# Retention and top-1 experts in one kernel: where the first expert's weights stand among the loads of queries, keys and values

## The chip, the core and the metric

The kernel runs on one core of a Trainium2 chip. The metric is the time of one execution on the device in microseconds (us). A core has five engines, each with an instruction stream of its own that it follows in order: TensorE (PE, products), VectorE (DVE), ScalarE (ACT), GpSimd (POOL) and SyncE (SP, which here only issues DMAs). DMAs are issued from SyncE, ScalarE and GpSimd and are carried by 16 DMA engines. Engines wait for each other, and for the landing of DMAs, by semaphores.

## The reference

Two parts, in float32. First retention over 8 batches, 8 heads, 576 positions, head size 64:

```python
scores = scale * np.matmul(q, k.transpose(0, 1, 3, 2))
Dmat = np.where(rel >= 0, gamma[:, None, None] ** rel[None, :, :], 0.0)
attn_out = np.matmul(scores * Dmat[None], v)
x = attn_out.transpose(0, 2, 1, 3).reshape(4608, 512)
```

Then a mixture of 8 experts on these 4608 tokens of 512 numbers. A token is computed only where its skip score is positive; then it goes to the expert with the greatest logit:

```python
do_compute = x @ w_skip > 0
e_idx = argmax(xc @ w_gate)          # xc: the tokens that are computed
h = np.maximum(xc[mask] @ w1[e], 0)  # 512 -> 1024
y[mask] = gate_w[mask, None] * (h @ w2[e])   # 1024 -> 512
out[do_compute] = xc + y
```

## The kernel before

**Retention, in 36 tiles.** A tile g is 128 positions of one batch (or 64 of each of two batches), all heads. Its queries, keys and values lie in one SBUF tile `u_g`, which two loads fill from `qkv`, each of 128 x 1024 numbers, 512 KB: `load_half(g, 0)` and `load_half(g, 2)` (the second is half as large for every ninth tile, the last one among them). There are 5 buffers for u. In round g of the loop, TensorE makes the scores of tile g + 1 (`psc`, `psq`), the state (`ps_s`) and the values (`pxt`) of tiles g and g - 1, and transposes what is finished (`px`); VectorE and ScalarE multiply by the decay and copy; GpSimd scales the keys (`kn`) and the values (`vs`). Round g asks for the second half of tile g + 3 behind a block of products, and for the first half of tile g + 4 at its end. ScalarE copies finished tokens to `xn` and writes them to `out` in DRAM.

**Routing beside it.** Each four tiles, logits are made, and from them VectorE makes a rank for each token (`route_a`, `route_b`, `slots`). After 24 tiles the expert with most tokens so far is chosen to go first (`choose_first`); its number is `lead_id`, and SyncE reads it into a register (L370), since the address of the weights depends on it. After 28 tiles `close_first` makes the list `gi` of this expert's first 256 tokens, and GpSimd gathers them from `out` into `xg0` by two indirect DMAs (L352).

**The first expert's weights** come in 8 chunks of 512 KB (`w_0_f`, f = 0 to 7; `load_w`, L161), each a piece of `w1` and a piece of `w2`. There are 4 buffers for raw chunks. A product in float32 is made of three products of parts: each chunk is split in a high part `whi` (a cast on ScalarE, L776) and a low part `wlo` (raw less high: on GpSimd in four pieces, L781, or on VectorE, L171). A buffer comes free when the low part is made. The loads of the first five chunks, AHEAD = 5, and their splits are asked for by `weights()`, once in each round from the time at which the register has its number. In each call one load is asked for. The split of a chunk is asked for two calls later, but no sooner than the gathers (`"first" in marks`), except for the first KFRONT chunks.

**Behind the loop** the gathered tokens are transposed (`pt_early`), split on ScalarE (`x`, L175) and VectorE (L176), and `up_early` multiplies them by chunks 0 to 2 (`ph_early`); the rest of the routing goes on between these. Then the experts follow one after the other, TensorE busy nearly without a break.

The order on TensorE is the order in which the code is written. The other engines are ordered by a scheduler, which keeps to dependencies, to what `keep_in_program_order` and `issue_after` pin, and to the order of the code otherwise.

Of the kernel before, what the change touches and what calls it, by code (L numbers as in the profile page):

```python
# [24 lines left out]
NT = NTOK // P  # L25
# [23 lines left out]
UAHEAD = UBUFS - LAG  # L49
# [7 lines left out]
NQD = P // QD  # L57
KCUT = 3
KRANK = 4
KFRONT = 1  # L60
KCOUNT = 3
CUT = 2 * P
EARLY = ("sc0", "sc1", "xt")
# [25 lines left out]
def kernel(  # L89
# [9 lines left out]
    nc = tc.nc  # L99
# [58 lines left out]
    def load_w(e, f, regs):  # L158

        t = wpool.tile([P, 2, NCC, P], F32, tag="w", name=f"w_{e}_{f}", bufs=4)  # L160
        marks["load"] = nc.sync.dma_start(t.rearrange("p m c i -> p (m c i)"), w[bass.ds(regs[e], 1), f].rearrange("o p c -> (o p) c"))  # L161
        return t

    def parts(t):
        return [wpool.tile([P, 2, NCC, P], F32R, tag=n, name=f"{n}_{t.name}") for n in ("whi", "wlo")]
# [287 lines left out]
    wq, hs, marks = {}, {}, {}  # L453
    regs = []
# [38 lines left out]
    with ExitStack() as actx:  # L493
# [19 lines left out]
        def load_half(g, s, after=None):  # L513
            if s == 0:
                u_t[g] = ap.tile([P, 4, NPR, P], F32, tag="u", name=f"u_{g}", bufs=UBUFS)
            n = 1 if s and g % NQ == HALF else 2
            half = nc.sync.dma_start(
                u_t[g][:, s : s + n].rearrange("p s a i -> p (s a i)"),
                qkv[g, s // 2, :, : n * DM],
            )  # L520
            if after is not None:
                tc.add_manual_dep(
                    half.ins,
                    after.name,
                    mybir.DependencyInfo(mybir.DependencyClass.Sync, mybir.DependencyReason.DATA),
                    reason="the second half begins behind a block of products",
                )
# [5 lines left out]
        for g, s in ((0, 0), (1, 0), (0, 2), (2, 0), (1, 2), (3, 0), (2, 2), (3, 2)):  # L533
            load_half(g, s)
            if (g, s) == (1, 2):
                nc.sync.dma_start(gt_sb[:, 0], gtab.rearrange("p (a q) -> p a q", a=NPR))
# [215 lines left out]
        added = []  # L752
        chunks = []
        held = []

        def queue_behind(piece, other):
            tc.add_manual_dep(
                piece.ins,
                other.ins.name,
                mybir.DependencyInfo(mybir.DependencyClass.NoSync, mybir.DependencyReason.DATA),  # L760
                reason="the first gathers are asked for in front of these",
            )

        def weights():

            if not regs:
                return
            n = len(chunks)
            chunks.append(None)
            if 0 <= n - 2 < AHEAD:  # L770
                held.append(n - 2)
            while held and (held[0] < KFRONT or "first" in marks):
                f = held.pop(0)
                t = chunks[f]
                hi, lo = wq[0, f] = parts(t)
                tc.keep_in_program_order(nc.scalar.copy(hi, t))  # L776
                behind = ranked[-1] if len(ranked) == len(GROUPS) - 1 else None
                for m in range(2):
                    for c in range(0, NCC, NCC // 2):
                        some = lambda x: x[:, m, c : c + NCC // 2]  # L780
                        piece = nc.gpsimd.tensor_tensor(some(lo), some(t), some(hi).bitcast(F32), ALU.subtract)  # L781
                        if f < KFRONT:
                            tc.keep_in_program_order(piece)
                        else:
                            queue_behind(piece, marks["first"])
                        if behind is not None:
                            tc.add_manual_dep(
                                piece.ins,
                                behind.ins.name,
                                mybir.DependencyInfo(mybir.DependencyClass.Sync, mybir.DependencyReason.DATA),  # L790
                                reason="VectorE's operations on the gates go first",
                            )
                            behind = None
            if n < AHEAD:
                chunks[n] = load_w(0, n, regs)

        def slots(t):
            slot_match(t)
# [58 lines left out]
        for g in range(NT):  # L857
# [6 lines left out]
            if g == GLATE:  # L864
                load_half(g + UAHEAD - 1, 0, last_product())
            if g and g + UAHEAD - 1 < NT:
                load_half(g + UAHEAD - 1, 2, last_product())
# [20 lines left out]
            if last >= 1:  # L888
                stage_c(last - 1)
            routing(0 if g == NT - 1 else 3 if g < starts[KCUT + 1] else 8)  # L890
            weights()
        g = NT
        if LAG:
# [6 lines left out]
        while len(chunks) < AHEAD + 2:  # L900
            weights()
# [512 lines left out]
```

## Time and profile before

| | |
|---|---|
| three runs | 389.59, 392.66, 393.16 us; median 392.66 |
| profiled execution | 390.34 us, span 388.6 us |
| busy: TensorE, VectorE, ScalarE, GpSimd | 95%, 71%, 47%, 39% of the span |
| moved by DMA | 106.15 MB, 273 GB/s in the mean |
| the tiles' loop ends, first expert begins | at about 143 us, 153 us of the span |

The span goes from the first to the last instruction; the time of the execution has 1.7 us around it. All times of day below are microseconds from the span's start. An engine's idle time costs only where it lies on the way to the end; TensorE is the engine with the most work.

### The profile page before, as it was taken

Reading aid. Unit: us, or ns where it says so; the run is one execution under the profiler, and the core shown is the slowest. Engines: PE = TensorE matmul, PEld = TensorE weight load, DVE = VectorE, ACT = ScalarE, POOL = GpSimd, SP = SyncE. Lnnn points to the kernel's source line nnn. Section 1 sums busy time; section 2 is a strip of 40 time slices with the busy share of each in tenths; the row PEclk is TensorE's granted clock in tenths of the full one; section 3 lists DMA queues with packets and bytes.
Section 4 is the critical chain, followed back from the end, with each engine's and each line's share of the span. In section 5 each row is a group of like instructions: output and inputs, shape, how many; then the busy total and the mean of one; then the engine's idle time right before and its main releaser. Section 6 shows DMA issues by size and latency. Waiting matters only on the chain. (4 is left out here: it accounts for less than half of the span.)

```text
span 388.6 us, 12328 instructions
## 1 busy us (share of the span) xinstructions
PE 367.6 (95%) x4886; PEld 334.5 (86%) x4886; DVE 276.0 (71%) x615; ACT 181.7 (47%) x369; POOL 152.5 (39%) x211
## 2 busy tenths in 40 slices
PE   7899998989999898999999999999999999999991
PEld 3678877777887776888899999999999999999991
DVE  3576677578579794877856767867878768687762
ACT  2464555355544576117445455445545545555311
POOL 5885855555475389260136000420322322002032
PEclk9999999999999999999999999999999999999997
DMA  8989997989999988257899768978899898776511
GB/s 305 404 281 375 394 351 270 347 299 341 320 359 331 313 319 260 63 128 252 261 317 262 264 212 276 327 228 303 275 278 329 249 336 313 233 253 228 142 68 61
DMA packets 49573, 106.15 MB, mean 273 GB/s; under 512 B 6102, under 2 KB 21206, under 8 KB 49511
## 3 DMA queue, kind: packets, MB, share of 16 engines
q1 hardware_dynamic: 40951, 85.81, 65.2%
q0 software_dynamic: 3232, 9.99, 7.9%
q10 hardware_dynamic: 5328, 9.52, 6.5%
q8 instruction: 40, 0.66, 0.7%
q14 instruction: 22, 0.18, 0.1%
HBM read 83.51 MB, written 22.28 MB: 272 GB/s over the span
## 5 line engine op out<-in xcount | busy, mean ns | idle before, releaser
L171 DVE TENSOR_TENSOR wlo_w<-w,whi_w 128x1024 fp32r<-128x1024 f32 x59 | 72.0, 1223 | 37.8 <-ACT whi_w L170 35.4
L170 ACT CAST whi_w<-w 128x1024 fp32r<-128x1024 f32 x59 | 61.7, 1050 | 33.1 <-PE py L465 32.4
L465 PE MATMUL py<-hlo,whi_w 128*128 128x336 f32 (+6 forms) x224 | 67.8, 303 | 0.0
L465 PE MATMUL ph<-xhi,wlo_w 128*128 128x336 f32 (+6 forms) x224 | 67.6, 302 | 0.0
L465 PE MATMUL ph<-xlo,whi_w 128*128 128x336 f32 (+6 forms) x224 | 67.5, 302 | 0.0
L465 PE MATMUL ph<-xhi,whi_w 128*128 128x336 f32 (+6 forms) x224 | 67.5, 301 | 0.0
L465 PE MATMUL py<-hhi,wlo_w 128*128 128x336 f32 (+6 forms) x224 | 67.5, 301 | 0.0
L465 PE MATMUL py<-hhi,whi_w 128*128 128x336 f32 (+6 forms) x224 | 67.4, 301 | 0.0
L1035 POOL DMA_INDIRECT out<-rs,sidx x17 | 21.2, 1245 | 84.0 <-DVE rs L1034 82.8
L624 POOL TENSOR_TENSOR vs<-u,tab_sb 64x256 f32<-64x256 f32 x72 | 46.7, 649 | 9.9 <-DMA u<-qkv 2.7
L602 POOL TENSOR_TENSOR kn<-u,tab_sb 128x512 f32<-128x512 f32 x32 | 33.8, 1057 | 42.5 <-DMA u<-qkv 18.9
L687 PE MATMUL pxt<-u,vs 128*64 128x128 f32 (+1 forms) x576 | 47.8, 269 | 1.6 <-issue 1.6
L473 ACT ACTIVATE hhi<-ph 128x336 fp32r<-128x336 f32 (+8 forms) x61 | 25.8, 423 | 45.3 <-PE ph L465 45.0
L590 DVE TENSOR_TENSOR u<-psc,tab_sb 64x256 f32<-64x256 f32 x72 | 30.3, 420 | 23.4 <-PE pxt L663 7.7
L594 ACT COPY u<-psc 64x256 f32<-64x256 f32 x64 | 23.4, 366 | 48.7 <-DVE u L590 45.6
L465 PEld LDWEIGHTS ph<-xhi,whi_w 128*128 128x128 f32 x224 | 42.3, 189 | 0.1
L465 PEld LDWEIGHTS py<-hlo,whi_w 128*128 128x128 f32 x224 | 42.2, 188 | 0.2 <-DVE hlo L474 0.2
L465 PEld LDWEIGHTS ph<-xlo,whi_w 128*128 128x128 f32 x224 | 42.3, 189 | 0.1
L465 PEld LDWEIGHTS py<-hhi,whi_w 128*128 128x128 f32 x224 | 42.3, 189 | 0.0
L465 PEld LDWEIGHTS ph<-xhi,wlo_w 128*128 128x128 f32 x224 | 42.3, 189 | 0.0
L465 PEld LDWEIGHTS py<-hhi,wlo_w 128*128 128x128 f32 x224 | 42.3, 189 | 0.0
L572 PE MATMUL psc<-u 64*64 64x128 f32 (+1 forms) x576 | 39.1, 272 | 2.3 <-DMA u<-qkv 2.1
(213 smaller groups left out, 780.7 us busy)
## 6 DMA issues: line engine op xcount, KB each, us to landing
u<-qkv SPq DMA_DIRECT2D x68, 512.0 KB, 6.6
w<-w SPq DMA_DIRECT2D x64, 512.0 KB, 5.5
out<-xn ACTq DMA_DIRECT2D x36, 256.0 KB, 5.8
hop<-xg SPq DMA_DIRECT2D x12, 256.0 KB, 5.2
xh<-hop SPq DMA_DIRECT2D x48, 64.0 KB, 4.9
hopy<-yp SPq DMA_DIRECT2D x24, 128.0 KB, 3.4
yr<-hopy SPq DMA_DIRECT2D x6, 512.0 KB
u<-qkv SPq DMA_DIRECT2D x4, 256.0 KB
```

The lines of the kernel that those rows point to most:

```text
L170: nc.scalar.copy(hi, t)
L171: nc.vector.tensor_tensor(lo, t, hi.bitcast(F32), ALU.subtract)
L465: nc.tensor.matmul(ps, x, y, start=first and n == 0, stop=last and n == 3 * len(terms) - 1)
L473: nc.scalar.activation(hi, ph, AF.Relu)
L572: nc.tensor.matmul(psc_t[g][c][halves[1 - j ^ c], a, : q.stop - q.start], u[halves[j], 1 - j, a, c * D : (c + 1) * D], u[halves[j], j, a, ...
L590: nc.vector.tensor_tensor(u_t[g][h, j, :, :D], near[h, :, :D], mt_sb[h].unsqueeze(1).broadcast_to([D, NPR, D]), ALU.mult)
L594: nc.scalar.copy(u_t[g][h, j, :, D:], near[h, :, D:])
L602: nc.gpsimd.tensor_tensor(kn_t[g].rearrange("p a (j i) -> p a j i", j=2), u_t[g][:, 3].rearrange("p a (j i) -> p a j i", j=2), tt_sb[:, k ...
L624: nc.gpsimd.tensor_tensor(vs_t[g][h, j], u_t[g][h, 2, :, j * D : (j + 1) * D], tt_sb[h, TV + g % NQ // 2, :].unsqueeze(2).broadcast_to([D, ...
L687: nc.tensor.matmul(pxt[halves[j], a, q], vs_t[g][:, j, a, :], u_t[g][:, j, a, q], start=False, stop=a == NPR - 1, skip_group_check=True,)
L1035: done = nc.gpsimd.indirect_dma_start(out=out, out_offset=bass.IndirectOffsetOnAxis(ap=idx, axis=0), in_=rs[:n], in_offset=None, bounds_ch ...
```

## The change

Three things. Loads of chunks are no longer issued one by one between the loads of u: chunks that are asked for are put in a list, `due`, and issued only from the round on that asks for the last half of u, behind that half (`issue_after(marks["half"])`). And KFRONT is 0: the split of chunk 0 stands no longer in front of the gathers but behind them, as those of the other chunks do.

```diff
-KFRONT = 1
+KFRONT = 0
...
-            half = nc.sync.dma_start(
+            half = marks["half"] = nc.sync.dma_start(
                 u_t[g][:, s : s + n].rearrange("p s a i -> p (s a i)"),
                 qkv[g, s // 2, :, : n * DM],
             )
...
         held = []
+        due = []
...
             if n < AHEAD:
-                chunks[n] = load_w(0, n, regs)
+                due.append(n)
+            while due and g + UAHEAD >= NT:
+                f = due.pop(0)
+                with tc.issue_after(marks["half"].ins):
+                    chunks[f] = load_w(0, f, regs)
```

The first place is SyncE at the last loads of u. The names are the tile's or the chunk's number and the buffer's (`u_33_2489` is tile 33, `w_0_0_2522` chunk 0 of the first expert); ISA sets an address from a register. Before:

```order
L517 DMA u_33_2489<-qkv 128x1024
L370 TENSOR_LOAD lead_id_125
L161 ISA
L161 DMA w_0_0_2522<-w 128x1024
L517 DMA u_33_2489<-qkv 128x1024
L517 DMA u_34_2602<-qkv 128x1024
L161 ISA
L161 DMA w_0_1_2633<-w 128x1024
L517 DMA u_34_2602<-qkv 128x1024
L517 DMA u_35_2693<-qkv 128x1024
L161 ISA
L161 DMA w_0_2_2719<-w 128x1024
```

SyncE in the changed kernel, from the same load on:

```order
L517 DMA u_33_2489<-qkv 128x1024 x2
L517 DMA u_34_2600<-qkv 128x1024 x2
L517 DMA u_35_2689<-qkv 128x1024
L517 DMA u_35_2689<-qkv 128x512
L370 TENSOR_LOAD lead_id_125
L161 ISA
L161 DMA w_0_0_2801<-w 128x1024
L161 ISA
L161 DMA w_0_1_2803<-w 128x1024
L161 ISA
L161 DMA w_0_2_2805<-w 128x1024
```

The reading of `lead_id` and three loads of weights have moved behind the five loads of u that stood between them. The load of chunk 4 needs the buffer of chunk 0.

The second place is GpSimd from the keys of tile 33 to the split of chunk 1, with the two gathers (`xg0<-out,gi0`). Before:

```order
L602 TENSOR_TENSOR kn_33_2669<-u_33_2489,tab_sb_146 128x512
L624 TENSOR_TENSOR vs_33_2689<-u_33_2489,tab_sb_146 64x256 x2
L781 TENSOR_TENSOR wlo_w_0_0_2522_2713<-w_0_0_2522,whi_w_0_0_2522_2712 128x256 x4
L602 TENSOR_TENSOR kn_34_2755<-u_34_2602,tab_sb_146 128x512
L624 TENSOR_TENSOR vs_34_2775<-u_34_2602,tab_sb_146 64x256 x2
L624 TENSOR_TENSOR vs_35_2874<-u_35_2693,tab_sb_146 64x256 x2
L352 DMA xg0_126<-out,gi0_2907 128x512 x2
L781 TENSOR_TENSOR wlo_w_0_1_2633_2918<-w_0_1_2633,whi_w_0_1_2633_2917 128x256 x4
```

GpSimd in the changed kernel:

```order
L602 TENSOR_TENSOR kn_33_2665<-u_33_2489,tab_sb_146 128x512
L624 TENSOR_TENSOR vs_33_2685<-u_33_2489,tab_sb_146 64x256 x2
L602 TENSOR_TENSOR kn_34_2742<-u_34_2600,tab_sb_146 128x512
L624 TENSOR_TENSOR vs_34_2762<-u_34_2600,tab_sb_146 64x256 x2
L624 TENSOR_TENSOR vs_35_2867<-u_35_2689,tab_sb_146 64x256 x2
L352 DMA xg0_126<-out,gi0_2900 128x512 x2
L782 TENSOR_TENSOR wlo_w_0_0_2801_2911<-w_0_0_2801,whi_w_0_0_2801_2910 128x256 x4
L782 TENSOR_TENSOR wlo_w_0_1_2803_2918<-w_0_1_2803,whi_w_0_1_2803_2917 128x256 x4
```

The four pieces of chunk 0's low part have moved behind the gathers.

The third place is ScalarE from the write of tile 31 to the copies of the gathered tokens (`x0`), in the changed kernel:

```order
L708 DMA out<-xn_31_2877 128x512
L777 CAST whi_w_0_0_2801_2910<-w_0_0_2801 128x1024
L777 CAST whi_w_0_1_2803_2917<-w_0_1_2803 128x1024
L777 CAST whi_w_0_2_2805_2924<-w_0_2_2805 128x1024
L192 ACTIVATE ex0_86<-ls_28_2974 128x4x8
L649 COPY sv_34_3002<-ps_s_163 128x256
L707 COPY xn_32_3010<-px_32_3005 128x512
```

Three casts stand in a row here. ScalarE goes on two rows later with chunk 3:

```order
L777 CAST whi_w_0_3_2807_3013<-w_0_3_2807 128x1024
L707 COPY xn_33_3043<-px_33_3038 128x512
L708 DMA out<-xn_33_3043 128x512
L777 CAST whi_w_0_4_2931_3046<-w_0_4_2931 128x1024
L707 COPY xn_34_3084<-px_34_3079 128x512
L175 CAST x0_127<-pt_early_0_3087 128x2x256
L708 DMA out<-xn_34_3084 128x512
L175 CAST x0_127<-pt_early_2_3094 128x2x256
```

Chunk 4's cast stands ahead of the copies of the gathered tokens, as it did before. The cast of chunk 0 stood ten rows further ahead before, behind the write of tile 29; the rows from chunk 1's cast on stand as they stood.

## Rows read from the trace of the kernel before

**Rows 1.** The page, part 1: busy us (share of the span) and instructions.

```profile
PE 367.6 (95%) x4886; PEld 334.5 (86%) x4886; DVE 276.0 (71%) x615; ACT 181.7 (47%) x369; POOL 152.5 (39%) x211
```

**Rows 2.** Timeline of TensorE, 130 to 154: start, us, instruction [idle before <-releaser].

```profile
130.73 0.28 PE L663 MATMUL pxt<-sq,u 64*64 64x64 f32 x4
...
134.86 0.33 PE L572 MATMUL psc<-u 64*64 64x128 f32 x2 [1.21 <-DMA u<-qkv]
...
140.00 0.28 PE L572 MATMUL psc<-u 64*64 64x64 f32 x2 [0.60 <-DMA u<-qkv]
...
150.37 1.10 PE L741 MATMUL pt_early<-ident,xg 128*128 128x128 f32 x7 [1.80 <-DMA xg<-out,gi]
...
153.02 0.48 PE L465 MATMUL ph_early<-x,whi_w 128*128 128x256 f32 x2
```

**Rows 3.** Timeline of SyncE, 118 to 156: DMAs that it issues.

```profile
124.95 0.36 SPq L161 DMA_DIRECT2D w<-w  x1
125.41 1.79 SPq L517 DMA_DIRECT2D u<-qkv  x2
...
133.61 0.33 SPq L517 DMA_DIRECT2D u<-qkv  x1
```

**Rows 4.** Waits of SyncE, 118 to 140: us in total, times, longest.

```profile
SPq L517 <- DMA u<-qkv: 3.2, 1, 3.2
...
SPq L370 <- DVE u L590: 2.6, 1, 2.6
```

**Rows 5.** Tile u, 123 to 142: issue to landing.

```profile
DMA to landing us min/median/max: 7.9/7.9/7.9
```

**Rows 6.** Stretches: busy us of each engine, granted clock, DMA share, GB/s.

```profile
124.00:130.00 6.00, 6.00 (x152) 5.36 (x152) 5.74 (x21) 2.54 (x7) 2.50 (x4) 1.00 0.77 224
130.00:142.00 12.00, 9.81 (x252) 8.04 (x250) 9.50 (x32) 7.97 (x17) 7.28 (x10) 1.00 1.01 389
```

**Rows 7.** Timeline of VectorE, 138 to 155.

```profile
140.89 0.44 DVE L344 TENSOR_SCALAR gi<-ids 128x2 int32<-128x2 f32 x1
...
151.64 1.29 DVE L176 TENSOR_TENSOR x<-pt_early,x 128x512 fp32r<-128x512 f32 x2 [3.16 <-ACT x L175]
```

**Rows 8.** Timeline of GpSimd, 130 to 160.

```profile
136.10 2.79 POOL L781 TENSOR_TENSOR wlo_w<-w,whi_w 128x256 fp32r<-128x256 f32 x4
...
142.21 1.29 POOL L624 TENSOR_TENSOR vs<-u,tab_sb 64x256 f32<-64x256 f32 x2 [0.91 <-DMA u<-qkv]
143.68 1.22 POOL L352 DMA_INDIRECT xg<-out,gi  x1 [0.17 <-POOL vs L624]
145.21 1.01 POOL L352 DMA_INDIRECT xg<-out,gi  x1 [0.31 <-DVE cb L207]
146.24 11.06 POOL L781 TENSOR_TENSOR wlo_w<-w,whi_w 128x256 fp32r<-128x256 f32 x16
```

**Rows 9.** Timeline of ScalarE, 130 to 153.5.

```profile
147.08 1.04 ACT L776 CAST whi_w<-w 128x1024 fp32r<-128x1024 f32 x1 [0.41 <-ACT xn L707]
148.53 0.58 ACT L707 COPY xn<-px 128x512 f32<-128x512 f32 x1 [0.40 <-DMA out<-xn]
151.03 0.58 ACT L175 CAST x<-pt_early 128x512 fp32r<-128x512 f32 x1 [1.92 <-PE pt_early L741]
```

**Rows 10.** Tile w, 90 to 180: issue to landing.

```profile
DMA to landing us min/median/max: 4.3/6.2/8.8
```

**Rows 11.** Tile w, 148 to 160: issue to landing.

```profile
DMA to landing us min/median/max: 4.3/4.3/4.3
```

**Rows 12.** Tile xg, 140 to 152: issue to landing of the two gathers.

```profile
DMA to landing us min/median/max: 4.5/4.8/5.1
```

**Rows 13.** Stretches at the end of the trace, columns as in Rows 6.

```profile
380.00:381.00 1.00, 0.86 (x8) 0.51 (x6) 0.98 (x2) 0.00 (x0) 0.00 (x0) 1.00 0.00 0
384.00:385.00 1.00, 0.00 (x0) 0.00 (x0) 0.00 (x0) 0.00 (x0) 0.47 (x1) 0.69 0.57 217
```

**Rows 14.** Timeline of TensorE, 0 to 9.

```profile
1.28 4.02 PE L117 MATMUL ps_m<-mc 128*128 128x512 bf16 x9 [1.28 <-DVE mc L111]
```

## The prediction, made before the changed kernel ran

> **What bounds the kernel now.** I read the page first: TensorE is busy for 367.6 of 388.6 us [rows 1], so almost any idle time of it that goes comes off the end, and any that is added goes on. The change touches only the stretch in which the last tiles of queries, keys and values meet the first expert, so I then read TensorE's timeline there. It has three idle times with a releaser of interest [rows 2]: 1.21 us before the scores of tile 34 and 0.60 us before those of tile 35, both for a load of u, and 1.80 us before the transposes of the first gathered tokens, for the gather. Together 3.61 us; that is the most that the change can give: 392.66 - 3.6 = 389.1 us.
>
> Why those loads of u are late is seen on SyncE's timeline and in its waits. SyncE stood 2.6 us for the value of lead_id [rows 4] before it issued the first weights at 124.95, and only behind that the second half of tile 33 and the first of tile 34 (126.87, the second of the pair) [rows 3]. That load landed 7.9 us later [rows 5], at 134.8, which is where the scores of tile 34 start. The second half of tile 35 had another wait of 3.2 us for a load to land [rows 4] and left at 133.61, though the products that it stands behind were over at 131.0 [rows 2]. In the table by stretch the DMA engines were 77% busy from 124 to 130 and full (1.01, 389 GB/s) from 130 to 142 [rows 6]: time was left unused, then everything came at once.
>
> **What is removed.** SyncE's order now has all of u in front of lead_id and the weights. The load of tile 34 leaves up to 2.6 us sooner and has one chunk less before it, which at 389 GB/s is 1.3 us; it needs 1.2 to be there in time. So the 1.21 goes. Tile 35's first half has two chunks less before it, 2.7 us, and needs 0.6 more than the 1.2 by which its user moves up; so that goes too. TensorE comes to the end of the tiles some 1.8 us sooner.
>
> **The gather moves more than that.** In the trace GpSimd could not ask for the gather until it had scaled the values of tile 35, which began at 142.21 behind a load of u; the first gather began at 143.68 [rows 8]. The list of tokens had been ready since 140.89 + 0.44 = 141.33 on VectorE [rows 7]. With u early, the list is ready about 1.2 sooner, at 140.1. The values: load at 131.0, landed 7.9 later at 138.9, 1.29 of work and 0.17 of wait [rows 8], so 140.4; were the load to take 8.8 [rows 10], 141.3. I take 140.5 for the first gather, 3.2 us sooner than now, between bounds of 140.1 and 141.3, and 143.7 if nothing of this comes true.
>
> **What is added: a chain that was hidden.** There are four buffers for raw chunks, so the fifth load waits until the low part of chunk 0 is made. Before, that was done at 136.10 + 2.79 = 138.9, in the shade of the tiles [rows 8]. Now it stands behind both gathers. And on ScalarE the high part of chunk 4 stands, as before, ahead of the copy of tile 34 and of the two copies that take the gathered tokens out of PSUM. Before, chunk 4 was there when ScalarE came to it: it was cast at 147.08, four microseconds before the tokens' copies at 151.03 [rows 9]. Now those copies wait for it. Counted from the start of the first gather, g:
> both gathers issued, 146.24 - 143.68 = 2.56; four subtractions, 2.79 [rows 8]; the fifth load to landing, see below, 4.6; cast 1.04, copy of tile 34 0.58, two copies of tokens of 0.58 each [rows 9]; the last subtraction on VectorE, half of 1.29 [rows 7], 0.65; and 0.09 until TensorE starts (152.93 to 153.02) [rows 2, 7]. Sum 13.5 us.
> With g = 140.5 the first products of the expert begin at 154.0; in the trace they begin at 153.02. So **1.0 us is lost**, although 3.6 us of idle time were there to be won.
>
> The landing of that load is the unknown. In the stretch the loads of weights took 4.3, 6.2 in the middle, 8.8 at most [rows 10]; the one that can be timed from 148 on, when the rush is over, took 4.3 [rows 11], and the gathers of that time 4.5 to 5.1 [rows 12]. The fifth load leaves at 140.5 + 5.35 = 145.9, beside the second gather and two writes of out; I take 4.6. With 4.3 and the earliest g the loss is 0.3; with 6.2 and the latest g it is 3.4.
>
> **What costs nothing, and under which cover.** The three casts of chunks 0 to 2 now stand in one row on ScalarE ahead of the copies of tiles 32 and 33; four loads in a row must land for them. That is covered: TensorE has to wait for the gather and then for the fifth chunk anyway. TensorE is ready at 142.0 (second gather) + 5.1 + 2.65 of work (150.37 to 153.02) = 149.8, so casts may run 4 us late before they count, except chunk 0, which must be cast when GpSimd is free at 143.1; a load that leaves at 132 and takes 8.8 has landed at 140.8 and is cast by 141.9. GpSimd makes five low parts in a row instead of four, 2.8 us more, but begins 3.2 sooner: the loads of chunks 5 to 7, which wait for these, stay where they are. ScalarE's copy of u for tile 33 no longer stands behind a cast, which takes up to 1.05 off VectorE's way to the list; that is in the 1.2. Behind 154 every engine does what it did, and TensorE is the bound to the end, so 1.0 stays 1.0.
>
> **The sum.** The profiled execution took 390.34, its span 388.6. With +1.0 it becomes 391.3. The three runs have a median of 392.66 (389.59 to 393.16), 2.3 above it, so against the median I forecast 392.66 + 1.0 = **393.7 us**.
>
> **Rivals.**
> *The clock falls.* TensorE now stands idle from about 149.8 to 154.0, 4.2 us. At the end of the trace its last product is in 380 to 381, and in 384 to 385 the granted clock is 0.69 in the mean [rows 13], so it fell from 2.4 to 1.2 GHz within four microseconds of idleness; the idle time of 1.80 was followed by no fall. How dear: the first nine products of the kernel took 4.02 us, 447 ns for 512 columns, which is the lower level [rows 14]; so at most half of 4.02, 2.0 us, until it is up again. The time is then 392.66 + 3.0 = 395.7. One fall in a trace doesn't tell whether 4.2 us will always do. The Trainium skill (TensorE: Matmul & The Clock Gate, section "HAM oscillation — how this bites in real kernels") speaks here against the change: it says that a wait for DMA between two bursts of products sends the engine back to half its clock. By that rule the forecast would be 395.7, without it 393.7; the trace agrees that idleness ends in a fall, not that this wait is long enough.
>
> *The gather comes no sooner (slower).* If the DMA engines are the true limit and u lands as late as now, g stays at 143.7, and the chain of 13.5 ends at 157.2: +4.2, or 396.8. For it speaks the share of 1.01 from 130 on, against it the 77% before [rows 6]. It decides from g = 139.5 on: each microsecond of g later than that is one lost.
>
> *The fifth chunk isn't the last to come (faster).* If the load lands so fast that the tokens' copies wait for the gather alone, TensorE starts at 149.8 and the time is 392.66 - 3.2 = 389.5. For this the load would have to land within half a microsecond; the shortest seen is 4.3. Smaller gains, to about -1, need g near 139 together with a landing of 4.
>
> **How the numbers follow.** Chances: forecast 0.60, clock 0.20, gather no sooner 0.12, faster 0.08. The runs shown differ by 0.9%, so about 1%, 3.9 us, is what a measurement of this kernel can tell from no change. Beyond it on the slow side lie the second rival, and the clock's fall where the load also takes 5.5 (392.66 + 1.9 + 2.0 = 396.6): 0.16. On the fast side hardly anything lies, since all idle time together is 3.6: 0.04. Within: 0.80. The range goes from 390.0, a small gain with the runs at their lower values, to 397.2, the latest g or the fallen clock.
>
> **What would show it.** In the profile after: no idle time for u before the scores of tiles 34 and 35; the first gather near 140.5; the fifth load of weights issued near 146; on ScalarE an idle time before the cast of chunk 4 that ends with its load, and the tokens' copies right behind; TensorE idle for some 4 us before ph_early; the granted clock tells the first rival. I am wrong if TensorE's products on ph_early begin before 152.5 or after 156.5, or if idle time moves to a place behind them.

## The result and the profile after

The changed kernel takes 393.24 us (median of 21 runs, 389.19 to 397.96) beside 390.28 for the kernel before (21 runs); the ratio is 1.0085 with a 95% interval of 1.0057 to 1.0113. Measured twice more, it came to 1.0040 (1.0002 to 1.0079) and 1.0064 (1.0029 to 1.0099). The kernel before, measured against itself in the same series as the 1.0040, gave 1.0027 (0.9983 to 1.0071), so that series alone tells little. By the three together the change costs 0.4 to 0.9%, some 1.6 to 3.3 us: slower, and within the 1% that the prediction set as its bound. The profile of the second measurement fell in an execution of 399.9 us, 6 us above its median, and is not used; its times are.

The profiled execution took 393.43 us, its span 391.7. TensorE's timeline around the place, the answer to [rows 2]:

```profile
135.89 0.33 PE L572 MATMUL psc<-u 64*64 64x128 f32 x2
...
140.59 0.27 PE L572 MATMUL psc<-u 64*64 64x64 f32 x2
...
143.95 0.33 PE L687 MATMUL pxt<-u,vs 128*64 128x128 f32 x2 [0.50 <-issue]
...
149.49 0.66 PE L705 MATMUL px<-ident,xt 128*128 128x128 f32 x4
149.98 1.13 PE L741 MATMUL pt_early<-ident,xg 128*128 128x128 f32 x8
...
152.58 0.22 PE L232 MATMUL ps_m<-mks,ones 128*128 128x24 bf16 x3
155.50 0.54 PE L465 MATMUL ph_early<-x,whi_w 128*128 128x256 f32 x2 [2.70 <-DVE x L176]
155.84 0.41 PE L465 MATMUL ph_early<-x,wlo_w 128*128 128x256 f32 x1
156.05 0.63 PE L465 MATMUL ph_early<-x,whi_w 128*128 128x256 f32 x2
```

The three idle times of [rows 2], 1.21 and 0.60 for u and 1.80 for the gather, are gone. In their place stands one of 2.70, for the gathered tokens. The two products with whi that follow take 0.63 us together. Before, they took 0.41:

```profile
153.46 0.41 PE L465 MATMUL ph_early<-x,whi_w 128*128 128x256 f32 x2
```

The granted clock shows why. Stretches of after, columns as in [rows 6] (length, then busy time of TensorE's products and weight loads, VectorE, ScalarE, GpSimd, then the clock):

```profile
149.00:155.40 6.40, 3.80 (x45) 2.67 (x45) 1.93 (x4) 3.29 (x6) 6.40 (x10) 1.00 0.78 244
155.80:159.20 3.40, 3.40 (x18) 3.40 (x17) 1.54 (x9) 1.17 (x2) 3.40 (x6) 0.50 0.94 313
159.30:162.00 2.70, 2.70 (x28) 2.65 (x28) 2.63 (x13) 0.61 (x2) 0.28 (x3) 1.00 0.13 52
```

The clock is at 2.4 GHz during the idle time, falls to 1.2 GHz a third of a microsecond after the products have begun, and stays there for 3.4 us.

Who was late is read backwards. VectorE's timeline (its list `gi`, as in [rows 7], and the last subtraction), then ScalarE's, the answer to [rows 9]:

```profile
141.79 0.17 DVE L344 TENSOR_SCALAR gi<-ids 128x2 int32<-128x2 f32 x1
...
154.16 1.29 DVE L176 TENSOR_TENSOR x<-pt_early,x 128x512 fp32r<-128x512 f32 x2 [3.86 <-ACT x L175]
```

```profile
147.90 0.58 ACT L707 COPY xn<-px 128x512 f32<-128x512 f32 x1
...
152.11 1.05 ACT L777 CAST whi_w<-w 128x1024 fp32r<-128x1024 f32 x1 [3.62 <-DMA w<-w]
153.06 0.58 ACT L707 COPY xn<-px 128x512 f32<-128x512 f32 x1
153.54 0.59 ACT L175 CAST x<-pt_early 128x512 fp32r<-128x512 f32 x1
```

ScalarE stood 3.62 us at the cast of chunk 4, with the copy of the last tile and both copies of tokens behind it. The load that it waited for left SyncE at 148.3 and landed 3.8 us later; two rows of the tile's answer for 147 to 150, and what SyncE waited for (118 to 150, the answer to [rows 4]):

```profile
L161 SPq DMA_DIRECT2D w<-w x1: 333/333/333, 148.3 to 148.3; - x1
...
DMA to landing us min/median/max: 3.8/3.8/3.8
```

```profile
SPq L161 <- POOL wlo_w L782: 4.7, 1, 4.7
...
SPq L370 <- DVE u L590: 0.4, 1, 0.4
```

It left late because chunk 0's buffer came free late. SyncE no longer stands 2.6 us for lead_id, only 0.4, but stands 4.7 for a low part. GpSimd, the answer to [rows 8]:

```profile
139.91 1.29 POOL L624 TENSOR_TENSOR vs<-u,tab_sb 64x256 f32<-64x256 f32 x2 [2.08 <-PE pxt L687]
142.89 1.22 POOL L352 DMA_INDIRECT xg<-out,gi  x1 [1.69 <-issue]
144.42 1.01 POOL L352 DMA_INDIRECT xg<-out,gi  x1 [0.31 <-issue]
145.44 13.78 POOL L782 TENSOR_TENSOR wlo_w<-w,whi_w 128x256 fp32r<-128x256 f32 x20
```

### The profile page after: what moved, and what is told of

Its sections match the earlier page's. It is cut to its first block, busy times and chain, and to the rows that moved or that the text cites. A ratio compares the mean times of both kernels' runs of the same rounds, so it can differ in the third digit from the quotient of the medians.

```text
span 391.7 us, 12328 instructions
## 1 busy us (share of the span) xinstructions
PE 370.7 (95%) x4886; PEld 336.9 (86%) x4886; DVE 275.9 (70%) x615; ACT 181.4 (46%) x369; POOL 152.4 (39%) x211
## 4 chain that ended last, share of the span: by engine, by line
PE 67%; DMA 15%; issue 10%; DVE 3%; POOL 2%; ACT 1%; SPq 1%; POOLq 0%; ACTq 0%
PE py L465 17%; PE ph L465 16%; DMA out<-rs,sidx 8%; PE pxt L687 7%; PE ps_s L638 5%; PE px L705 5%; PE psc L572 5%; PE pxt L663 3%; DMA u<-qkv 2%; PE pl L713 2%; PE psq L572 2%; DMA xg<-out,gidx 2%; PE pn L728 1%; PE ph_early L465 1%; DMA tab_sb<-tab 1%
## 5 line engine op out<-in xcount | busy, mean ns | idle before, releaser
L624 POOL TENSOR_TENSOR vs<-u,tab_sb 64x256 f32<-64x256 f32 x72 | 45.6, 633 | 9.8 <-PE pxt L687 3.1
L572 PE MATMUL psc<-u 64*64 64x128 f32 (+1 forms) x576 | 40.1, 273 | 0.9 <-issue 0.9
```

The source lines that it names most:

```text
L572: nc.tensor.matmul(psc_t[g][c][halves[1 - j ^ c], a, : q.stop - q.start], u[halves[j], 1 - j, a, c * D : (c + 1) * D], u[halves[j], j, a, ...
L624: nc.gpsimd.tensor_tensor(vs_t[g][h, j], u_t[g][h, 2, :, j * D : (j + 1) * D], tt_sb[h, TV + g % NQ // 2, :].unsqueeze(2).broadcast_to([D, ...
```

## The experiments

One table serves them all. It has the starts of five of TensorE's instructions in each profile: the scores of tile 28 (up to there TensorE's instructions are the same in all kernels), those of tile 35, the transposes of tile 34 (the last ahead of the gathered tokens), the first product of `ph_early`, and the first product of the second expert; then the last less the first, and the ratio of the times with its interval.

| kernel | tile 28 | tile 35 | tile 34 turned | ph_early | second expert | 28 to second | ratio |
|---|---|---|---|---|---|---|---|
| before | 110.00 | 140.00 | 147.67 | 153.02 | 189.79 | 79.8 | |
| c0, before again | 111.74 | 141.24 | 149.62 | 154.51 | 191.40 | 79.7 | 1.0027 (0.9983 to 1.0071) |
| after | 111.33 | 140.59 | 149.49 | 155.50 | 193.83 | 82.5 | 1.0085 (1.0057 to 1.0113) |
| d4, after again | 110.29 | 140.12 | 148.48 | 154.79 | 193.30 | 83.0 | 1.0064 (1.0029 to 1.0099) |
| e1, filler | 110.50 | 139.50 | 147.84 | 155.14 | 192.03 | 81.5 | 1.0081 (1.0050 to 1.0112) |
| e2, cast behind | 112.03 | 141.25 | 150.85 | 154.02 | 191.44 | 79.4 | 1.0044 (1.0007 to 1.0080) |
| e3, own buffer | 113.55 | 141.96 | 152.13 | 155.30 | 192.15 | 78.6 | 1.0032 (0.9993 to 1.0070) |
| d1, e2 and e3 | 112.95 | 142.46 | 151.93 | 155.10 | 192.68 | 79.7 | 1.0026 (0.9985 to 1.0068) |
| e4, split only | 111.56 | 141.35 | 149.54 | 156.78 | 196.19 | 84.6 | 1.0173 (1.0123 to 1.0222) |
| d2, e4 and own buffer | 112.80 | 141.38 | 150.35 | 153.52 | 191.60 | 78.8 | 1.0047 (1.0017 to 1.0077) |
| d3, d2 and cast behind | 113.01 | 142.49 | 150.48 | 155.97 | 194.06 | 81.1 | 1.0060 (1.0023 to 1.0097) |
| c2, loads spread | 114.62 | 143.50 | 151.85 | 156.94 | 195.32 | 80.7 | 1.0065 (1.0028 to 1.0103) |
| c3, loads only | 109.99 | 140.95 | 149.51 | 153.00 | 189.92 | 79.9 | 1.0037 (1.0001 to 1.0073) |

From the second expert on all are alike (191.0 to 191.3 us to the last product, 192.5 in d1); behind the last product 6.4 to 8.3 us more follow (7.8 in before, 6.8 in c0, 6.9 in after). Tile 28 begins anywhere from 110.0 to 114.6, and at two different times in the two profiles of the kernel before, so a difference of total times of single profiles says little; the column "28 to second" says more. It has one profile for each experiment; the two of before are 0.1 us apart, those of after 0.5.

**Theory and rivals.** The theory is the prediction's: the split of chunk 0 behind the gathers makes chunk 4's load late, and ScalarE meets its cast ahead of the tokens. Rivals: the loss is the clock's fall alone; it is the four loads in a row; or it lies ahead of the place, where the profile of before was faster by 1.3 us.

**e1: is it the clock?** After, with eight filler products ahead of the first `up_early`. They add work and change no result.

```diff
+        fill = pp.tile([P, 512], F32, tag="sc1", name="fill")
+        for _ in range(8):
+            nc.tensor.matmul(fill, ones, ones.unsqueeze(1).broadcast_to([P, 4, P]), start=True, stop=True)
         up_early(0)
```

> The changed kernel with eight products of 128x512 (bf16, on a matrix of ones, result used by nobody) on TensorE ahead of the first ph_early, in the idle time of 2.70 us that its trace shows there. My theory: of the loss of 0.85% a part is the fallen clock (the trace of the changed kernel shows half clock for 3.4 us right behind that idle time). Then the granted clock stays at 1.00 from 150 to 165, the products of ph_early run at their full pace (0.36 us per group of three against 0.64), and the ratio to the kernel before is 1.0085 less 1.4 us of 390, about 1.005. Rival, the fall is a consequence of something else or costs nothing since VectorE sets the pace there: ratio stays at 1.008 to 1.009.

Timeline of e1, and the stretch in which the clock of after was down:

```profile
151.00 1.89 PE L912 MATMUL fill<-ones 128*128 128x512 bf16 x8
155.14 0.51 PE L465 MATMUL ph_early<-x,whi_w 128*128 128x256 f32 x2 [2.25 <-DVE x L176]
155.48 0.28 PE L465 MATMUL ph_early<-x,wlo_w 128*128 128x256 f32 x1
155.60 0.41 PE L465 MATMUL ph_early<-x,whi_w 128*128 128x256 f32 x2
```

```profile
155.80:159.20 3.40, 3.40 (x31) 3.40 (x30) 3.19 (x14) 1.16 (x3) 2.99 (x7) 1.00 0.85 336
```

The clock stays up (1.00 in place of 0.50), and from `ph_early` to the second expert it takes 36.9 us, in place of 38.3 in after and 38.5 in d4. So the fall costs 1.5 us; before has 36.8 and 36.9. The 28-to-second time is 1.0 and 1.5 shorter than in the profiles of after, and still 1.8 longer than before: the clock is about half of the loss. The time itself, 1.0081, is the rival's figure (1.008 to 1.009), not the theory's 1.005: it doesn't show the gain, 0.4%, which is less than the width of the interval.

**e2 and e3: is it the cast of chunk 4, and its buffer?** In e2 chunk 4's split is asked for behind the copies of the tokens; in e3 it has a raw buffer of its own, so that its load waits for no one (a small tile, `gtr`, gets one buffer in place of two, for room).

```diff
-            while held and (held[0] < KFRONT or "first" in marks):
+            while held and "first" in marks and (held[0] < AHEAD - 1 or "turned" in marks):
...
         up_early(0)
+        marks["turned"] = True
+        weights()
```

```diff
-                    chunks[f] = load_w(0, f, regs)
+                    own = ac.tile([P, 2, NCC, P], F32, tag="w4", name="w_own") if f == AHEAD - 1 else None
+                    chunks[f] = load_w(0, f, regs, own)
```

> The changed kernel, but the split of chunk 4 is asked for behind the copies of the gathered tokens and the first ph_early, so that on ScalarE the tokens' copies no longer stand behind the cast that waits for the fifth load. My theory, that this place makes the loss: TensorE begins ph_early 2.7 us sooner against the last tile than in the changed kernel, the clock doesn't fall, and 2.7 + 1.4 = 4.1 us come back: ratio to before 0.998 (0.995 to 1.001). Rival, the loss lies in the rush of four weight loads on the last tiles: the ratio stays at 1.008, and the idle time goes elsewhere.

> The changed kernel, but chunk 4 has a raw buffer of its own, so that its load doesn't wait for the low part of chunk 0; the order on ScalarE is that of the changed kernel. My theory (the fifth load is late only because it waits for that buffer): it is issued right behind the fourth, near 138, has landed by 147, the cast of chunk 4 doesn't wait, and TensorE begins ph_early when the gather allows: as in the run before, ratio 0.998. Rival 1, a fifth load in the rush delays the last tiles or the gather: TensorE's wait moves to the gather, ratio near 1.003. Rival 2, the place isn't it: 1.008.

ScalarE in e2, where the copies of tokens come right behind that of the tile, and in e3, where the cast is still ahead of them but waits for no load:

```profile
151.54 0.59 ACT L707 COPY xn<-px 128x512 f32<-128x512 f32 x1 [1.70 <-PE px L705]
152.02 0.59 ACT L175 CAST x<-pt_early 128x512 fp32r<-128x512 f32 x1
```

```profile
151.54 1.05 ACT L777 CAST whi_w_own<-w_own 128x1024 fp32r<-128x1024 f32 x1 [0.41 <-ACT xn L707]
152.82 0.58 ACT L707 COPY xn<-px 128x512 f32<-128x512 f32 x1 [0.24 <-PE px L705]
153.31 0.59 ACT L175 CAST x<-pt_early 128x512 fp32r<-128x512 f32 x1
```

In both, `ph_early` follows the turned tile 34 by 3.17 us (6.0 and 6.3 in after, 5.3 and 4.9 in before), TensorE does not wait, the clock stays up. The whole loss of the stretch is gone: 79.4 and 78.6. That shows the chain: buffer, load, cast, copies. The times came out worse than the theories, which had 0.998 for both: 1.0044, and 1.0032, the figure of e3's first rival. What e2 and e3 win at this point over before, some 2 us, they lose ahead of it: from the scores of tile 35 to the turned tile 34 they take 9.6 and 10.2 us, before and c0 7.7 and 8.4. TensorE stands in the middle of a block of products, in e2 for

```profile
145.31 0.33 PE L687 MATMUL pxt<-u,vs 128*64 128x128 f32 x2 [1.61 <-issue]
```

and in e3 for 1.52, waiting for nothing that the profile shows; this is taken up by c2. The rest of what their times are above before lies outside the stretch (see c0).

**e4: the split alone.** Before, with KFRONT at 0; the loads stay between those of u.

```diff
-KFRONT = 1
+KFRONT = 0
```

> The kernel before with one part of the change alone, the split of chunk 0 behind the gathers; the loads stand where they stood. My theory: the fifth load waits for chunk 0's low part here too, and now without the earlier gather: first gather near 143.7 minus the 1 us that ScalarE no longer spends on a cast in between at best, ph_early 13.5 later, that is 3 to 4 us later than before, and the clock falls as well: ratio 1.010 to 1.014, worse than the change as a whole. Rival, that the moved loads make the loss: ratio near 1.000.

ScalarE, and the stretch behind the first products:

```profile
153.38 1.04 ACT L776 CAST whi_w<-w 128x1024 fp32r<-128x1024 f32 x1 [4.84 <-DMA w<-w]
```

```profile
155.70:162.40 6.70, 5.62 (x26) 5.62 (x27) 4.48 (x19) 2.51 (x5) 5.54 (x11) 0.50 0.66 235
```

This half alone loses more than the whole: ScalarE waits 4.84 us, TensorE 3.67, the clock is down for 6.8 us, and the time is 1.7% longer, more than the 1.0 to 1.4% expected.

**c3: the loads alone.** After with KFRONT at 1 (and the loads asked for ahead of the splits within `weights()`, since the first split is asked for in the same call).

```diff
-KFRONT = 0
+KFRONT = 1
```

> The changed kernel with KFRONT at 1: the loads stand behind those of u, but the split of chunk 0 stays in front of the gathers (the other half of the change alone). Theory: ScalarE waits for chunk 0 (landing about 139.5) ahead of its copies for tile 35, some 2.3 us, and GpSimd makes 2.8 us of low part ahead of the last values and the gathers, so the gathers are asked for about 2 us later than in after; chunk 4's buffer comes free 5 us sooner and its cast waits no more. From tile 31 to the second expert 69 to 71 us, 392 to 394.5 us in all. Rival: chunk 4's load was all that made the change slower, the earlier wait costs nothing, and this gives 67 us and about 391.

The rival was right (67.2 us from tile 31 to the second expert, 391.53 in all). ScalarE and GpSimd do wait for chunk 0 ahead of tile 35 (the row below is TensorE, at the scores of tile 35), but there is no wait for chunk 4, `ph_early` follows tile 34 by 3.5 us, and the stretch is 79.9, that of before.

```profile
140.95 0.27 PE L572 MATMUL psc<-u 64*64 64x64 f32 x2 [1.43 <-ACT lt L722]
```

So by the stretch the loads behind u win nothing by themselves, and all of the loss comes with the split. The times alone do not show it: in this series c3 has 1.0037, after 1.0040, and the kernel before itself 1.0027.

**c0: is it chance that before was ahead at tile 28?** The same kernel once more.

> The kernel before, unchanged. In the profiles so far the scores of tile 28 begin at 110.0 us in before and at 110.5 to 113.6 in after and the four experiments, though TensorE's instructions are the same up to there; the idle of TensorE that no release explains ('issue') up to tile 31 is 3.3 us in before and 3.3 to 5.6 in the others. If that is chance, this second profile of before begins tile 28 anywhere between 110 and 113.5, and the ratio to before is 1.000 within its interval. If the changed programs are slower from the start, it begins tile 28 at 110.0 within 0.5.

Tile 28 begins at 111.74 this time, c3 and d4 begin it at 109.99 and 110.29: that before was ahead of after was chance. For the kernels with a remedy chance is not shown. All six profiles of them (e2, e3, and c2, d1, d2, d3 below) begin tile 28 at 112.0 or later, the seven others at 111.7 or sooner; two of the six, d1 and c2, have a fall of the clock on the way. Whether a remedy makes the kernel slower there, which would explain the ratios above 1 of e2, e3, d1 and d2 beside stretches no longer than before's, no run tells. The waits for u that the change is about are a matter of this chance too. TensorE in c0:

```profile
136.34 0.33 PE L572 MATMUL psc<-u 64*64 64x128 f32 x2 [0.45 <-DMA u<-qkv]
...
151.85 1.11 PE L741 MATMUL pt_early<-ident,xg 128*128 128x128 f32 x7 [1.46 <-DMA xg<-out,gi]
```

Where [rows 2] have 1.21 and 0.60, there are 0.45 and none. The three other kernels whose loads stand between those of u show the same spread: none in e4 and d2, 1.22 in d3. What could be won here was nothing to 1.8 us from one execution to the next.

**c1 and d4: after again.**

> The changed kernel, unchanged. Theory: from the scores of tile 31 to the first product of the second expert it takes 69.6 us again (before: 67.8), with 2.7 us of idle time in front of the first products of the gathered tokens and the clock fallen behind it; what lies ahead of tile 31 is chance and may come out 0 to 2 us shorter. Time 391.5 to 393.5, ratio 1.005 to 1.010. Rival: the fall of the clock was a matter of that one execution; then 68.2 us and 391 to 392.

> The changed kernel, unchanged, a third profile. 82.5 to 83.5 us from the scores of tile 28 to the second expert as in the first two, with 2.4 to 2.7 us of idle time ahead of the first products of the gathered tokens and the clock fallen for 3.41 us right behind it; ratio 1.003 to 1.010. Rival: without a fall of the clock it is 81 us and a ratio under 1.004.

c1 gave 393.57 us, the ratio 1.0040 as above, less than expected. The profile of d4 is that of after again, with 3.00 us of idle time, more than expected, and the clock down from 154.85 on for 3.41 us:

```profile
154.79 0.78 PE L465 MATMUL ph_early<-x,whi_w 128*128 128x256 f32 x2 [3.00 <-DVE x L176]
```

The mean granted clock of the timed runs fits a fall there in most executions, not in all: its median is 0.995 for before, 0.990, 0.991 and 0.990 for the three measurements of after, 0.9945 for e1, 0.994 to 0.995 for e2, e3, d1, d2 and c3, and 0.9875 for e4. A fall of 3.4 us is 0.5 x 3.4 / 391 = 0.004. The mean doesn't tell where the clock fell.

**c2: are the four loads in a row to blame for the 1.6 us?** e2, with each of the loads of chunks 1 to 3 held until another round's products are done, and chunks 2 and 3 split behind the tokens as well.

```diff
+                if f:
+                    tc.add_manual_dep(
+                        marks["load"].ins,
+                        last_product().name,
...
+                if n < AHEAD + 1:
+                    break
...
-            while held and "first" in marks and (held[0] < AHEAD - 1 or "turned" in marks):
+            while held and "first" in marks and (held[0] < 2 or "turned" in marks):
```

> The kernel of e2 (cast of chunk 4 behind the token copies), with the loads of chunks 1 to 3 each held until the products of another round are done, in place of four loads in a row, and the splits of chunks 2 and 3 behind the token copies too. Theory: with four loads of weights in a row, TensorE stood still for 1.61 us at 145.3 in e2 and 1.52 in e3 in the middle of a block of products that waited for no one, 1.4 us behind the landing of a 16 KB packet of its instructions; without the rush this stall is under 0.3 us, the stretch from tile 31 to the second expert falls from 67.2 to 65.6 us, and the time from 392.4 to about 390.9. Rival: the loads have nothing to do with that stall, it stays at 1 us or more, and the time stays at 392.4. Third: chunk 2's late split holds up its products, and the time goes up.

The stall at that place is gone, and the time is no shorter all the same (1.0065 beside 1.0044). None of the three outcomes came as put: the wait moved to ScalarE, whose copy needs a buffer that an earlier write to `out` still reads.

```profile
154.50 0.59 ACT L707 COPY xn<-px 128x512 f32<-128x512 f32 x1 [3.79 <-DMA out<-xn]
```

Whether the loads in a row cause the stall stays open. With four in a row it was 0.50 and 0.36 (after, d4), 1.61 (e2), 1.52 (e3), 1.48 (d1), but under 0.2 in e1 and c3; without, 0.84 in d2 and 0.2 or less in before, c0, e4, d3 and c2.

**d1, d2, d3: does a mended version beat before?** d1 has both remedies. d2 is e4 with the buffer of its own, d3 is d2 with the cast behind the tokens; their edits are those of e2 and e3.

> The changed kernel with both remedies: chunk 4 has a raw buffer of its own (e3), and its split is asked for behind the copies of the gathered tokens (e2). From the scores of tile 28 to the first product of the second expert it takes 79.4 us with e2, 78.6 with e3, 82.5 in after, 79.8 and 79.7 in the two profiles of before. Theory: either remedy alone already takes the whole wait away (3.17 us from the last transposes of the tiles to the first products of the gathered tokens in both), so both together give 78.5 to 79.5 us, no fallen clock, and a time within 1% of before (ratio 0.996 to 1.004). Rival: each leaves a part, and both give under 78 us and a ratio under 0.996.

> The kernel of e4 (before with the split of chunk 0 behind the gathers, the loads of weights still between those of queries, keys and values), with a raw buffer of its own for chunk 4. e4 takes 84.6 us from the scores of tile 28 to the second expert. Theory: all that e4 loses comes from chunk 4's load, which waits for the buffer of chunk 0; with a buffer of its own this is 78.5 to 80 us, the clock does not fall, and the time is within 1% of before. Rival: the late low part itself holds up the first products; then it stays over 82 us and over 1% slower.

> d2 with chunk 4's split behind the token copies as well. Theory: the same as d2 within 0.7 us (78.5 to 79.5 us in the stretch, ratio 0.996 to 1.004). Rival: without the four loads in a row, TensorE does not stand still behind tile 35's scores (1.5 to 1.6 us in e2 and e3), and this is the version that beats before: 77.5 us and a ratio under 0.996.

None is shown to. d1 is as e2 and e3, 79.7 and 1.0026. d2 shows once more that e4's loss was the buffer: 78.8 in place of 84.6, 3.17 us from tile 34 to `ph_early`; its ratio, 1.0047, is clear of 1. Neither d3's theory nor its rival came true: 81.1 us. In d3 waits as in before are back, 1.22 for u and

```profile
153.32 1.11 PE L741 MATMUL pt_early<-ident,xg 128*128 128x128 f32 x7 [2.06 <-DMA xg<-out,gi]
```

for the gather. d2, whose loads stand in the same places, has neither. In e2, d1, d2 and d3 the way from `ph_early` to the second expert is 0.6 to 1.3 us longer than in before, with no fall of the clock; TensorE waits 0.46 to 0.99 us there for the routing (`mks`, VectorE).

## Why the prediction was right, and where it was not

It said 393.7 us in a range of 390.0 to 397.2, no difference beyond 1%; measured were 393.24 and ratios of 1.004 to 1.0085. The chain is the one that it named; the fall of the clock on top of it was one of its rivals, not the forecast. The sizes are not as forecast: it expected 1.0 us of loss above a median of 392.66, and the loss is larger, 3.0 us in the stretch (82.5 and 83.0 against 79.8 and 79.7), while that median of three runs was high: 390.28 in 21 runs. The two errors nearly cancel in the time; that the forecast lies 0.5 us from the measured median is luck. By its steps:

- *The waits for u go.* No wait for u is left there in any profile with the loads behind u, and in after SyncE stands 0.4 in place of 2.6 for lead_id. But e4 and d2 have none either, with the loads where they stood, so the moved loads are not shown to be needed for it. *TensorE comes to the end of the tiles some 1.8 us sooner*: wrong. From tile 28 to the scores of tile 35 it takes 29.3 and 29.8 us in after and d4, 30.0 and 29.5 in before and c0: 0.2 in the mean. One reason is that the 1.8 was one execution's (0.45 in c0), the other that idle time which waits for nothing shown is larger: in that stretch 1.6 and 2.6 us in after and d4, 1.0 and 1.7 in before and c0. And behind it, up to the turned tile 34, 0.6 more is lost.
- *The first gather 3.2 us sooner, at 140.5.* Mis-sized: 142.89. Counted from tile 28 it is 31.6 and 32.0 in after and d4 against 33.7 and 33.5 in before and c0, 1.8 us sooner. The values were no hindrance (done at 141.20), the list was: 141.79 + 0.17 = 141.96, in place of the 140.1 that the prediction took. And the gather began only 0.93 us behind the list; in all seven profiles of the table in which the list comes last (after, d4, e1, e2, e3, d1, c2) it is 0.93 or 0.94. The prediction had no such term: it counted only the 0.17 from values to gather.
- *The fifth load waits for chunk 0's low part; ScalarE's cast of it holds up the tokens.* Right, shown by e2, e3 and d2, which each cut the chain at another link.
- *13.5 us from the gather to the first products.* 12.61 in after and 12.46 in d4. The load took 3.8 in place of 4.6; the rest is as summed.
- *Three casts in a row cost nothing.* Neither shown nor disproved: products of after wait 0.33 us behind ScalarE there, but those of c0, without the row, wait 0.64 at the same place.
- *TensorE is ready at 149.8 and stands for some 4 us.* It is ready at 152.8, since the tiles end later, and stands for 2.70. With g mis-sized by 2.4 and the chain by -0.9, `ph_early` begins at 155.5, not 154.0: within the bounds that the prediction set itself (152.5 to 156.5).
- *The clock falls*, a rival with a chance of 0.20 and a price of up to 2.0 us. It is what happened in both profiles, and the price is some 1.5. The prediction took its measure from the end of the trace and judged a fall unlikely, at 4.2 us of idle time; it came at 2.70. The Trainium skill's rule, which it cited (TensorE: Matmul & The Clock Gate, "HAM oscillation — how this bites in real kernels"), that a wait between two bursts of products sends the clock to half, came true here: 0.50 from 155.8 on. The waits of the page's example are longer than this one, and not every wait here was followed by a fall: 1.80 us in before and 2.06 in d3 were not. The forecast's 1.0 for the chain (measured 1.4: 44.2 and 44.5 us from tile 28 to `ph_early` in after and d4, against 43.0 and 42.8 in before and c0) and the rival's 2.0 (measured 1.6) together are the 3.0 that was lost.
- *The gather comes no sooner* and *the fifth chunk isn't the last*: neither came true. The second is what e3 makes of the kernel, and its gain was not there either: 78.6 against 79.7, and a ratio of 1.0032.

## What to carry to other kernels

Before a step is moved behind something else, look for who waits for the buffer that it frees: here one constant moved four subtractions from 136.1 to 145.4 us, and the price was paid by the load of the fifth chunk and by an engine on which that chunk's cast stood ahead of urgent copies. If the step has to move, an order that asks for the cast behind the copies, or one more buffer, takes the wait away; that it also makes the kernel as fast as it was is not shown (1.0026 to 1.0047 in e2, e3, d1 and d2). And an idle time that one profile shows is not yet there to be won: take a second profile of the same kernel. Here the waits for u were 1.81, 0.45, none, none and 1.22 us in five profiles with the loads in the same places.

## What the runs showed of the hardware

**Instructions come late.** In each profile TensorE stands still 5 to 11 times for 0.2 to 2.6 us for nothing that is shown ("issue"), 3 to 7 us in all, and all of it in the tiles. If its products and weight loads are numbered in order of their start, most of these stalls lie a multiple of about 253.5 apart: 1457, 2217, 3231, 3485, 5259 in before, 1455, 2215, 3229, 3483, 5257 in e2. The DMA queues of after, whose columns are packets, MB and share of the time, have a queue of

```profile
q8 instruction: 40, 0.66, 0.6%
```

for 9,772 products and weight loads, one packet of 16 KB for each 244. In e2 the packet that belongs to the stall of 1.61 us came in from 142.92 to 143.92, and TensorE went on at 145.31. So these are most likely waits for instructions; no experiment changed the instructions to test it. The Trainium skill (Runtime: NRT & Kernel Launch, "Instruction fetch mechanics") gives blocks of 16 KB, 256 instructions, with which the trace agrees, and calls the cost of passing from one to the next mostly hidden. If these stalls are that cost, it is not hidden in these tiles, where a block lasts for only 4 to 7 us and the DMA engines are nearly full, and the measurement decides. Such stalls are a part of what makes tile 28 begin anywhere from 110.0 to 114.6 us: up to there they sum to 1.6 us in c3 (109.99) and 4.7 in d2 (112.80).

**The length of the idle time alone doesn't decide on the clock.** It fell within 0.4 us after idle times of 1.90 (c2 at 84.09, d1 at 39.33), 2.70 (after) and 3.00 us (d4), for 3.4 us each, and 1.1 us ahead of the end of one of 3.67 (e4), for 6.8. It did not fall behind 1.90 in d3, 2.06 in d3, 2.25 in e1 (with 1.89 us of fillers ahead of it), nor behind the longest of these stalls, in d2:

```profile
34.70 0.33 PE L705 MATMUL px<-ident,xt 128*128 128x128 f32 x1 [2.56 <-issue]
```

```profile
34.70:38.00 3.30, 3.30 (x85) 2.89 (x86) 1.62 (x5) 0.83 (x2) 1.22 (x2) 1.00 0.74 263
```

**A load out of the rush is quick.** Chunk 4's 512 KB landed in 3.8 us in after, less than any load of weights from 90 to 180 of the kernel before [rows 10]; the one that can be timed of the four in a row ahead of it took 7.4.
